# Splitting the last block's V load 3/8 and 5/8 around its K load in a single-core decode attention

## Chip, cores and metric

One core of one Trainium2 chip runs the whole kernel. The metric is the device time of one execution in microseconds (us), as the median of several runs; lower is better. Three runs of the kernel before gave 1286.35, 1285.47 and 1285.8 us, so the median is 1285.8 us.

## What is computed

One token (a row x of 448 numbers) attends to a cache of 65,536 keys. There are 16 query heads and 8 key/value heads of width 256, so each K/V head serves two query heads. A small gated side branch (a layer norm, a gelu and one reduction) is mixed in at the end. Cut to what matters, the reference is:

```python
q = (x @ wq).reshape(B, Sq, 16, 256).transpose(0, 2, 1, 3)
k = jnp.repeat(k_cache, 2, axis=1)            # k_cache: (1, 8, 65536, 256) bf16
v = jnp.repeat(v_cache, 2, axis=1)            # v_cache: the same shape
scores = jnp.einsum("bhqd,bhkd->bhqk", q, k) * (256 ** -0.5)
p = softmax(scores, axis=-1)
o = jnp.einsum("bhqk,bhkd->bhqd", p, v)
a = o.transpose(0, 2, 1, 3).reshape(1, 1, 4096) @ wo
g = sigmoid((x * gate_w).sum(-1, keepdims=True))
return g * a + (1 - g) * b                    # b: the side branch, (1, 1, 448)
```

Almost all bytes are K and V: 8 heads x 65,536 keys x 256 numbers x 2 bytes = 268 MB each.

## The kernel before

**Blocks.** The keys are cut into 32 blocks of 16,384 (four per head), numbered n = 0 to 31 in one loop (line 495); `L` is 31, the last. In a block, each of the 128 partitions holds 128 successive keys ("rows" below, index j). K comes in two halves of 64 rows, 4 MiB each, into two tiles `kn0` and `kn1` (`load_k`, line 106). V comes into one tile `vt` of 128 rows, 8 MiB (`load_v`, line 113). Neither is double-buffered: a tile is loaded again when its last reader is done. All these loads are issued by the SyncE queue (SP) in an order written out by hand.

**Scores of a block** (`score_block`, line 352). A block is 32 groups, t = 0 to 31. A group (`transposes`, line 325) is four TensorE transposes of 128x128 fp32 words (each word is a pair of bf16 numbers) from a K tile into one PSUM bank, and one VectorE copy of that bank to `kT` (line 334). Groups 0 to 15 read `kn0`, groups 16 to 31 read `kn1`. After every fourth group, two batches of four score matmuls (line 343) follow, two and three groups late. `hooks` is a table from t to a function that is called after group t: this is how other work is put among the transposes.

**Softmax** (line 380) is a chain of short steps between VectorE, TensorE and ScalarE. It ends in `p_sb` and its transpose `pT`. There are two `pT` tiles, so block n - 1's may still be read while block n is scored.

**Products with V.** A quarter of a block's products (`pv(n, ip)`, line 366; ip = 0 to 3) is 16 matmuls. Quarter ip reads rows 32 ip to 32 ip + 31 of `vt`. `accumulate` (line 416) then folds the result into `acc` on VectorE.

**Order for ordinary blocks.** Scores of n; issue V of n and both K halves of n + 1; softmax of n; products of n.

**Order around the end.** This is what the change touches. It runs over the last but one block (30) and the last (31):

- After the scores of block 30, SP issues: the first half of V of block 30 (rows 0 to 63), K of block 31 into `kn0` and `kn1`, then the second half of V of block 30 (rows 64 to 127) (lines 511 to 514). Then comes the softmax of block 30, with no products behind it.
- The scores of block 31 carry hooks (line 501): after group 4 a small VectorE step (`result_base`), after group 8 quarter 0 of block 30's products, after group 14 quarter 1.
- V of block 31 is loaded into the K tiles in six pieces of 64, 32, 16, 8, 4 and 4 rows, each as soon as the transposes that read those rows are done (`load_v_last`, line 121).
- After the softmax of block 31 come four small matmuls (line 527), then quarters 2 and 3 of block 30's products (lines 531 and 532), one small matmul (line 533) and `accumulate`.
- Block 31's own products run the other way round (line 552): V is the stationary operand, in 256 short matmuls over the rows j in order. After row 63 the accumulated result `acc` is added by eight fp32 matmuls (`collect`, lines 437 and 559). Then the result is scaled, projected (line 565), copied (line 571) and written out (line 572).

TensorE's instructions run in program order (`seq` writes that order down), and so do SP's issues. The two lines of the order that matter most here:

```python
            score_block(n, {4: result_base, 8: lambda: pv(L - 1, 0), 14: lambda: pv(L - 1, 1)})
...
            load_v(n, 0, KP)
            load_k(L, 0)
            load_k(L, 1)
            load_v(n, KP, VP)
```

Of the kernel before, what the change touches and what calls it, by code (L numbers as in the profile page):

```python
# [20 lines left out]
VP = BLK // 128  # L21
KP = VP // 2
NJ = 16
NI = VP // NJ
# [4 lines left out]
def kernel(  # L29
# [28 lines left out]
    def seq(ins):  # L58
        e = ins.ins.engine
        if e in last:  # L60
            tc.add_manual_dep(
                ins.ins,
                last[e],
                mybir.DependencyInfo(
                    mybir.DependencyClass.NoSync, mybir.DependencyReason.DATA
                ),
                reason="program order",
            )
        last[e] = ins.ins.name
        return ins  # L70
# [31 lines left out]
    def rows(cache, n):  # L102
        g, b = divmod(n, NB)
        return cache[0, g, b * BLK:(b + 1) * BLK, :].rearrange("(p j) d -> p j d", j=VP)

    def load_k(n, h, pieces=((0, KP),)):
        for j0, j1 in pieces:
            seq(nc.sync.dma_start(
                out=k_tiles[h][:, j0:j1, :],
                in_=rows(A_k_cache, n)[:, h * KP + j0:h * KP + j1, :],  # L110
            ))

    def load_v(n, j0=0, j1=VP):
        seq(nc.sync.dma_start(out=vt[:, j0:j1, :], in_=rows(A_v_cache, n)[:, j0:j1, :]))

    def pairs(ap):
        return ap.rearrange("p (i j) d -> p i j d", i=2)
# [3 lines left out]
    def load_v_last(n):  # L121
        for j0, j1 in LAST:
            seq(nc.sync.dma_start(
                out=k_tiles[j0 // KP][:, j0 % KP:(j1 - 1) % KP + 1, :],
                in_=rows(A_v_cache, n)[:, j0:j1, :],
            ))
# [198 lines left out]
    def transposes(i, quarter):  # L325
        tp = tps[state["t"] % 4]
        state["t"] += 1
        for jj in range(4):
            seq(nc.tensor.transpose(  # L329
                tp[:, jj * 128:(jj + 1) * 128],  # L330
                k_tiles[i // 4][:, i % 4 * NJ + quarter * 4 + jj, :].bitcast(FP32),
                ident_f[:, :],
            ))
        seq(nc.vector.tensor_copy(  # L334
            out=kT_tiles[i % 2][:, quarter * 4:(quarter + 1) * 4, :, :].rearrange(
                "p j n c -> p (j n c)"
            ),
            in_=tp[:, :].bitcast(BF16),
        ))

    def scores(g, i, c):
        for a in range(4):
            seq(nc.tensor.matmul(  # L343
                sc_ps[32 * a:32 * (a + 1), :],
                lhsT=qpad[:, c, g, i, :],
                rhs=kT_tiles[i % 2][:, :, 32 * a:32 * (a + 1), c],
                start=(i == 0 and c == 0),
                stop=(i == NI - 1 and c == 1),
                tile_position=(0, 32 * a),
            ))  # L350

    def score_block(n, hooks={}):
        due = []
        for t, (i, quarter) in enumerate((i, q) for i in range(NI) for q in range(4)):
            transposes(i, quarter)
            if due and due[0][0] <= t:
                scores(n // NB, *due.pop(0)[1])
            if quarter == 3:
                due.append((t + 2, (i, 0)))
                due.append((t + 3, (i, 1)))  # L360
            if t in hooks:
                hooks[t]()
        while due:
            scores(n // NB, *due.pop(0)[1])

    def pv(n, ip):
        pT = pT_tiles[n % 2]
        for jj in range(NJ):
            grp = jj % 4
            seq(nc.tensor.matmul(  # L370
                pv_ps[32 * grp:32 * grp + 2 * REP, :, :],
                lhsT=pT[:, 32 * jj + 2 * REP * ip:32 * jj + 2 * REP * (ip + 1)],
                rhs=pairs(vt[:, 32 * ip:32 * (ip + 1), :])[:, :, jj, :],
                start=(ip == 0 and jj < 4),
                stop=(ip == NI // 2 - 1 and jj >= NJ - 4),
                tile_position=(0, 32 * grp),
            ))


    def softmax(n):  # L380
        b = n % NB
        nb, nb_old = nb_tiles[n % 2], nb_tiles[(n + 1) % 2]
        al, pT = al_tiles[n % 2], pT_tiles[n % 2]
        seq(nc.vector.tensor_reduce(out=rmax[:], in_=sc_ps[:, :], op=ALU.max, axis=AXIS.X))  # L384
        seq(nc.tensor.transpose(sm_ps[0:1, 0:128], rmax[:, 0:1], ident_f[:, :]))  # L385
        seq(nc.vector.tensor_reduce(  # L386
            out=(mrun if b == 0 else mnew)[:],
            in_=sm_ps[0:1, 0:128].rearrange("o (a i r) -> o r a i", a=4, r=REP)[:, :, :, 0:NI],
            op=ALU.max, axis=AXIS.XY,
        ))  # L390
        if b > 0:
            seq(nc.vector.tensor_tensor(out=mrun[:], in0=mrun[:], in1=mnew[:], op=ALU.max))  # L392
        seq(nc.tensor.matmul(  # L393
            sm_ps[:, 128:128 + REP], lhsT=ones_f[0:1, :], rhs=mrun[0:1, :], start=True, stop=True
        ))
        seq(nc.vector.tensor_tensor_reduce(  # L396
            out=junk[:], in0=sm_ps[:, 128:128 + REP], in1=nval[:], scale=1.0, scalar=0.0,
            op0=ALU.mult, op1=ALU.add, accum_out=nb[:, 0:1],
        ))
        seq(nc.scalar.activation(  # L400
            out=p_sb[:, :], in_=sc_ps[:, :], func=ACT.Exp, scale=scale,
            bias=nb[:, 0:1], accum_out=den[:, 0:1],
        ))
        if b > 0:
            seq(nc.scalar.activation(
                out=al[:], in_=nb_old[:], func=ACT.Exp, scale=-1.0, bias=nb[:, 0:1]
            ))
        seq(nc.vector.transpose(out=pT[:, :], in_=p_sb[:, :]))  # L408
        if b > 0:
            seq(nc.vector.scalar_tensor_tensor(  # L410
                out=lsum[:], in0=lsum[:], scalar=al[:, 0:1], in1=den[:], op0=ALU.mult, op1=ALU.add
            ))
        else:
            seq(nc.vector.tensor_copy(out=lsum[:], in_=den[:]))
# [52 lines left out]
    L = NBLK - 1  # L467

    def products(n):
        for ip in range(NI // 2):  # L470
            pv(n, ip)
        accumulate(n)
# [22 lines left out]
    for n in range(NBLK):  # L495
        if n == 0:
            score_block(n, {8: gate_sum, 20: mixer_tail})
        elif n < L:
            score_block(n, {5: gate_column, 16: last_wo} if n == 1 else {})
        else:  # L500
            score_block(n, {4: result_base, 8: lambda: pv(L - 1, 0), 14: lambda: pv(L - 1, 1)})
        if n < L - 1:
            load_v(n)
            load_k(n + 1, 0)
            load_k(n + 1, 1)
            if n == 0:
                seq(nc.sync.dma_start(
                    out=wo_sb[:], in_=A_wo.rearrange("(h p c) n -> p h c n", p=128, c=2)
                ))
        elif n == L - 1:  # L510
            load_v(n, 0, KP)
            load_k(L, 0)
            load_k(L, 1)
            load_v(n, KP, VP)
        else:
            load_v_last(L)
        softmax(n)
        if n == L:
            seq(nc.vector.tensor_scalar(
                out=esc[:], in0=fst[:], scalar1=al_tiles[L % 2][:, 0:1], scalar2=None, op0=ALU.mult  # L520
            ))
            seq(nc.vector.tensor_scalar(
                out=lsv[:], in0=val[:], scalar1=lsum[:, 0:1], scalar2=None, op0=ALU.mult
            ))
            f_ps = tps[0][:, 0:NCOL]
            for k in range(NCOL):
                seq(nc.tensor.matmul(  # L527
                    f_ps[:, k:k + 1], lhsT=base[0:1, k, :],
                    rhs=ones_f[0:1, 0:1], start=(k == 0), stop=False, skip_group_check=True,
                ))  # L530
            pv(n - 1, 2)
            pv(n - 1, 3)
            seq(nc.tensor.matmul(
                hd_ps[:, 456:456 + REP], lhsT=ones_f[:, :], rhs=lsv[:, :], start=True, stop=True
            ))
            accumulate(n - 1)
            seq(nc.vector.reciprocal(out=rdv[:], in_=hd_ps[:, 456:456 + REP]))
            seq(nc.vector.tensor_scalar(
                out=rdv[:], in0=rdv[:], scalar1=gcol[:, 0:1], scalar2=None, op0=ALU.mult
            ))  # L540
        if n < L - 1:
            if n % NB == NB - 1:
                denominators()
            products(n)
            if n % NB == NB - 1:
                head_end(n // NB)
# [56 lines left out]
```

## Time and profile before

| what | value |
|---|---|
| median of three runs | 1285.8 us (1285.47 to 1286.35) |
| the profiled execution's own time | 1285.52 us |
| its span in the profile | 1283.7 us |
| mean granted TensorE clock | 0.862 |
| TensorE matmul busy | 975.9 us, 76% |
| VectorE busy | 756.1 us, 59% |
| read from HBM | 544.22 MB, 424 GB/s over the span |
| DMA busy, slices 1 to 39 of 40 | 90% or more each |

The profiled execution lies 0.28 us under the median of the three runs, and 1.8 us of it lie outside the span. The granted clock is the share of full speed at which TensorE was let run; in this trace it is either 1 or 0.5 at any moment. "Landing" is the moment when the last of a load's sixteen completions was recorded. A line such as `kn<-in_A_k_cache_dram` names a load by its destination tile and its source. Lines with L329 are transposes, L343 score matmuls, L370 products of block 30 and earlier, L552 the products of block 31.

### The profile page before, as it was taken

What the parts mean: (1) busy time and instruction counts of PE and PEld (TensorE: products, weight loads), DVE (VectorE), ACT (ScalarE), POOL (GpSimd) and SP (SyncE); (2) the same over time, 40 slices, a digit from 0 to 9 for tenths busy, and PEclk for the clock granted to TensorE, in tenths of its full rate; (3) what the DMA queues carried; (4) which work ended last, traced back from release to release, by engine and by line L of the source; (5) the groups of instructions that cost most, each with busy time, mean ns of one, the idle gap of its engine ahead of it and who ended that gap; (6) DMA issues with size and microseconds to landing.
All of it is one profiled execution on the core that took longest, in us unless ns stands there. A gap on an engine that the chain in (4) does not pass through costs nothing.

```text
span 1283.7 us, 20141 instructions
## 1 busy us (share of the span) xinstructions
PE 975.9 (76%) x8761; PEld 639.8 (50%) x8761; DVE 756.1 (59%) x1360; ACT 44.9 (3%) x111; POOL 6.3 (0%) x9
## 2 busy tenths in 40 slices
PE   5767777787768888777877788877788767878677
PEld 4444444554445554445554455644455444455455
DVE  6565555665556655556654566645576555676563
ACT  4000000000000000000000000000000000000000
POOL 1000000000000000000000000000000000000000
PEclk9888888988888887888887888878889888898887
DMA  9999999999999999999999999999999999999996
GB/s 409 422 430 428 440 419 433 432 435 434 440 418 435 438 434 430 431 427 434 437 436 438 421 430 434 437 432 431 434 427 436 437 437 423 427 420 438 398 403 255
DMA packets 17838, 545.51 MB, mean 425 GB/s; under 512 B 2260, under 2 KB 4310, under 8 KB 4822
## 3 DMA queue, kind: packets, MB, share of 16 engines
q1 hardware_dynamic: 17312, 544.22, 98.6%
q8 instruction: 68, 1.11, 0.3%
q14 instruction: 20, 0.16, 0.0%
q10 hardware_dynamic: 438, 0.01, 0.0%
HBM read 544.22 MB, written 0.00 MB: 424 GB/s over the span
## 4 chain that ended last, share of the span: by engine, by line
DMA 68%; PE 30%; DVE 2%; issue 0%; DVEq 0%
DMA kn<-in_A_k_cache_dram 67%; PE tps L329 23%; PE sc_ps L343 5%; DVE kT L334 1%; PE pv_ps L370 0%; PE hd_ps L552 0%; PE sm_ps L552 0%; DMA xr<-in_A_x_dram 0%; PE tps L527 0%; PE hd_ps L440 0%; PE sm_ps L440 0%; DVE acc L418 0%; DVE rmax L384 0%; DVE z L278 0%; PE tps L565 0%
## 5 line engine op out<-in xcount | busy, mean ns | idle before, releaser
L334 DVE COPY kT<-tps 128x1024 bf16<-128x1024 bf16 x1024 | 647.1, 685 | 184.2 <-PE tps L329 183.2
L329 PE MATMUL tps<-ident_f,kn 128*128 128x128 f32 x4096 | 603.6, 296 | 108.4 <-DMA kn<-in_A_k_cache_dram 108.4
L329 PEld LDWEIGHTS tps<-ident_f,kn 128*128 128x128 f32 x4096 | 486.8, 151 | 228.8 <-DMA kn<-in_A_k_cache_dram 122.0
L370 PE MATMUL pv_ps<-vt,pT 128*4 128x512 bf16 x1984 | 172.9, 524 | 94.6 <-DMA vt<-in_A_v_cache_dram 90.8
L343 PE MATMUL sc_ps<-kT,qpad 128*32 128x512 bf16 x2048 | 201.0, 393 | 28.2 <-DVE kT L334 28.1
L370 PEld LDWEIGHTS <-pT 128*4 128x4 bf16 x1984 | 58.3, 108 | 195.3 <-issue 132.6
L418 DVE SCALAR_TENSOR_TENSOR acc<-acc,al,pv_ps 128x512 f32<-128x512 f32 x23 | 17.2, 748 | 160.5 <-PE pv_ps L370 160.5
L343 PEld LDWEIGHTS <-qpad 128*32 128x32 bf16 x2048 | 52.9, 93 | 110.8 <-issue 101.7
L400 ACT ACTIVATE p_sb<-sc_ps,nb 128x512 bf16<-128x512 f32 x32 | 22.0, 687 | 1178.4 <-DVE nb L396 1178.4
L423 DVE COPY acc<-pv_ps 128x512 f32<-128x512 f32 x8 | 5.5, 692 | 58.6 <-PE pv_ps L370 58.6
L408 DVE STREAM_TRANSPOSE pT<-p_sb 128x512 bf16<-128x512 bf16 x32 | 22.8, 712 | 28.9 <-ACT p_sb L400 28.9
L384 DVE TENSOR_REDUCE rmax<-sc_ps 128x1 f32<-128x512 f32 x32 | 22.1, 691 | 23.2 <-PE sc_ps L343 23.2
L385 PE MATMUL sm_ps<-ident_f,rmax 128*1 128x128 f32 x32 | 8.8, 276 | 25.4 <-DVE rmax L384 25.4
L393 PE MATMUL sm_ps<-mrun,ones_f 1*128 1x2 f32 x64 | 14.1, 288 | 14.2 <-DVE mrun L392 11.7
L385 PEld LDWEIGHTS sm_ps<-ident_f,rmax 128*1 128x1 f32 x32 | 2.5, 79 | 41.5 <-DVE rmax L384 41.5
L393 PEld LDWEIGHTS sm_ps<-mrun,ones_f 1*128 1x128 f32 x64 | 11.4, 221 | 20.4 <-DVE mrun L392 16.5
L396 DVE CUSTOM_DVE_ANT_0 junk<-sm_ps,nval 128x2 f32<-128x2 f32 x32 | 5.1, 159 | 17.1 <-PE sm_ps L393 17.1
L426 PE MATMUL hd_ps<-lsum,same 128*128 128x1 f32 x14 | 4.1, 362 | 13.9 <-DVE lsum L410 13.9
L426 PEld LDWEIGHTS hd_ps<-lsum,same 128*128 128x128 f32 x14 | 3.5, 311 | 14.5 <-DVE lsum L410 14.5
L386 DVE TENSOR_REDUCE mnew<-sm_ps 1x2 f32<-1x64 f32 x24 | 5.1, 213 | 8.9 <-PE sm_ps L385 8.9
L440 PE MATMUL hd_ps<-esc,acc 128*128 128x2 f32 x32 | 5.4, 274 | 6.0 <-DVE acc L418 6.0
L440 PEld LDWEIGHTS hd_ps<-esc,acc 128*128 128x128 f32 x32 | 4.8, 211 | 9.6 <-DVE acc L418 9.6
(99 smaller groups left out, 138.0 us busy)
## 6 DMA issues: line engine op xcount, KB each, us to landing
kn<-in_A_k_cache_dram SPq DMA_DIRECT2D x63, 4096.0 KB, 26.8
vt<-in_A_v_cache_dram SPq DMA_DIRECT2D x2, 4096.0 KB, 27.4
kn<-in_A_k_cache_dram SPq DMA_DIRECT2D x2, 2048.0 KB, 11.7
kn<-in_A_v_cache_dram SPq DMA_DIRECT2D x1, 4096.0 KB, 14.2
wo_sb<-in_A_wo_dram SPq DMA_DIRECT2D x1, 3584.0 KB
vt<-in_A_wq_dram SPq DMA_DIRECT2D x1, 3072.0 KB, 10.4
kn<-in_A_v_cache_dram SPq DMA_DIRECT2D x1, 2048.0 KB, 13.6
kn<-in_A_v_cache_dram SPq DMA_DIRECT2D x1, 1024.0 KB, 13.4
```

The source lines that it names most:

```text
L329: seq(nc.tensor.transpose(tp[:, jj * 128:(jj + 1) * 128], k_tiles[i // 4][:, i % 4 * NJ + quarter * 4 + jj, :].bitcast(FP32), ident_f[:, :],))
L334: seq(nc.vector.tensor_copy(out=kT_tiles[i % 2][:, quarter * 4:(quarter + 1) * 4, :, :].rearrange("p j n c -> p (j n c)"), in_=tp[:, :].bi ...
L343: seq(nc.tensor.matmul(sc_ps[32 * a:32 * (a + 1), :], lhsT=qpad[:, c, g, i, :], rhs=kT_tiles[i % 2][:, :, 32 * a:32 * (a + 1), c], start=( ...
L370: seq(nc.tensor.matmul(pv_ps[32 * grp:32 * grp + 2 * REP, :, :], lhsT=pT[:, 32 * jj + 2 * REP * ip:32 * jj + 2 * REP * (ip + 1)], rhs=pair ...
L384: seq(nc.vector.tensor_reduce(out=rmax[:], in_=sc_ps[:, :], op=ALU.max, axis=AXIS.X))
L385: seq(nc.tensor.transpose(sm_ps[0:1, 0:128], rmax[:, 0:1], ident_f[:, :]))
L393: seq(nc.tensor.matmul(sm_ps[:, 128:128 + REP], lhsT=ones_f[0:1, :], rhs=mrun[0:1, :], start=True, stop=True))
L400: seq(nc.scalar.activation(out=p_sb[:, :], in_=sc_ps[:, :], func=ACT.Exp, scale=scale, bias=nb[:, 0:1], accum_out=den[:, 0:1],))
L408: seq(nc.vector.transpose(out=pT[:, :], in_=p_sb[:, :]))
L418: seq(nc.vector.scalar_tensor_tensor(out=acc[:], in0=acc[:], scalar=al_tiles[n % 2][:, 0:1], in1=pv_ps[:, :, :], op0=ALU.mult, op1=ALU.add,))
L426: seq(nc.tensor.matmul(hd_ps[:, 460:461], lhsT=same[:].rearrange("p a r -> p (a r)"), rhs=lsum[:, 0:1], start=True, stop=True,))
L440: seq(nc.tensor.matmul(o_ps[c], lhsT=acc[:, e, :].rearrange("p (d c) -> p c d", c=2)[:, c, :], rhs=weights[:, e, :], start=(start and e == ...
```

## The change

The first piece of block 30's V load takes 48 rows (3/8 of 128) instead of 64, the second takes 80 rows instead of 64. Quarter 1 of block 30's products reads rows 32 to 63, so it needs both pieces; it is no longer called after group 14 and runs after the softmax of block 31 instead, ahead of quarters 2 and 3. Nothing is computed differently, and no instruction is added or removed: on TensorE, 16 weight loads and 16 matmuls stand later in the order; on SP, two loads have other sizes; the orders of the other engines are the same.

```diff
@@ -498,7 +498,7 @@
         else:
-            score_block(n, {4: result_base, 8: lambda: pv(L - 1, 0), 14: lambda: pv(L - 1, 1)})
+            score_block(n, {4: result_base, 8: lambda: pv(L - 1, 0)})
         if n < L - 1:
             load_v(n)
             load_k(n + 1, 0)
@@ -508,10 +508,10 @@
         elif n == L - 1:
-            load_v(n, 0, KP)
+            load_v(n, 0, 48)
             load_k(L, 0)
             load_k(L, 1)
-            load_v(n, KP, VP)
+            load_v(n, 48, VP)
         else:
             load_v_last(L)
         softmax(n)
@@ -528,8 +528,8 @@
-            pv(n - 1, 2)
-            pv(n - 1, 3)
+            for ip in range(1, NI // 2):
+                pv(n - 1, ip)
             seq(nc.tensor.matmul(
                 hd_ps[:, 456:456 + REP], lhsT=ones_f[:, :], rhs=lsv[:, :], start=True, stop=True
             ))
```

## Prediction

> **What bounds the kernel now.** I read the page's chain first, then the same chain in order of time over the last 80 us, then SP's issues with their times to landing, then the clock in stretches of 2 us, then the timeline of the tail.
>
> The page's shares of the chain say that the transfers bound the kernel:
>
> ```profile
> DMA 68%; PE 30%; DVE 2%; issue 0%; DVEq 0%
> ```
>
> In order of time (start, duration, what), the end of the chain is another matter:
>
> ```profile
> 1215.87 19.33 DMA kn<-in_A_k_cache_dram
> 1235.25 5.38 PE tps L329 x24
> ...
> 1243.06 0.97 PE pv_ps L370 x16
> ...
> 1248.57 0.86 PE pv_ps L370 x16
> ...
> 1265.26 3.35 PE pv_ps L370 x32
> ```
>
> The last DMA in the chain is block 31's first K half, landing at 1215.87 + 19.33 = 1235.20. From there to the end every step is TensorE or what it waits for, so whatever brings that landing forward, or shortens TensorE's work behind it, moves the end. The next view is the tail's timeline (start, duration, engine, line):
>
> ```profile
> 1269.51 0.16 PE L552 MATMUL hd_ps<-pT,kn 128*128 128x2 bf16 x1 [0.63 <-DVE rdv L537]
> ...
> 1272.78 0.99 PE L440 MATMUL hd_ps<-esc,acc 128*128 128x2 f32 x4
> ...
> 1274.28 3.68 PEld L552 LDWEIGHTS <-kn 128*128 128x128 bf16 x128
> ```
>
> Block 31's products start at 1269.51, pause for `collect`, and end at 1274.28 + 3.68 = 1277.96; 5.8 us of scaling, projection and output follow. How far this can move forward is set by the last V pieces. The queue's own timeline gives the issues:
>
> ```profile
> 1215.87 11.16 SPq L108 DMA_DIRECT2D kn<-in_A_k_cache_dram  x2
> 1227.08 0.43 SPq L114 DMA_DIRECT2D vt<-in_A_v_cache_dram  x1
> 1250.05 11.33 SPq L123 DMA_DIRECT2D kn<-in_A_v_cache_dram  x6
> ```
>
> The second and the third of them again, with bytes and time to landing:
>
> ```profile
> vt<-in_A_v_cache_dram SPq DMA_DIRECT2D x1, 4096.0 KB, 27.4
> kn<-in_A_v_cache_dram SPq DMA_DIRECT2D x1, 4096.0 KB, 14.2
> ```
>
> V's second half, issued at 1227.08, lands at 1254.5; block 31's first V piece, issued at 1250.05, at 1264.2; the last piece (issued at 1260.9, 13.4 us to landing on the page) at 1274.3. Last the clock (third column from the right):
>
> ```profile
> 1229.00:1231.00 2.00, 0.51 (x3) 0.29 (x2) 0.53 (x4) 0.70 (x3) 0.00 (x0) 0.92 0.99 381
> 1239.00:1241.00 2.00, 2.00 (x12) 1.33 (x10) 1.84 (x3) 0.00 (x0) 0.00 (x0) 0.52 1.18 508
> 1263.00:1265.00 2.00, 1.43 (x11) 1.24 (x11) 0.56 (x5) 0.48 (x1) 0.00 (x0) 0.96 0.94 401
> 1267.00:1269.00 2.00, 1.88 (x22) 0.59 (x11) 0.37 (x1) 0.00 (x0) 0.00 (x0) 0.69 0.99 416
> 1271.00:1273.00 2.00, 2.00 (x76) 2.00 (x73) 0.00 (x0) 0.00 (x0) 0.00 (x0) 0.66 0.36 134
> ```
>
> As the clock is 1 or 0.5, a mean of 0.92 over 2 us is a step 1.68 us in. So it drops at 1230.68, rises at 1240.92, drops at 1264.84, rises at 1268.24 and drops at 1271.64. The gaps (10.24, 23.92, 3.40, 3.40) are all whole multiples of 3.41: the clock is decided on a grid. TensorE slows after a mostly idle stretch of the grid and recovers after a busy one: idle from 1230.0 to 1235.25, busy from then, full speed only at 1240.92.
>
> **The change, term by term** (against the profiled execution, span 1283.7, own time 1285.52, 0.28 under the median of the runs).
>
> *1. K lands earlier.* 1 MiB of V moves from ahead of K to behind it. From 1235.20 to 1264.2, 12 MiB land (second K half, V's second half, block 31's first V piece): 29.0 / 12 = 2.42 us per MiB. From block 30's first K half (1177.45 + 27.79 = 1205.24) to 1235.20 it is 29.96 / 12 = 2.50. I take **-2.42** (bounds -2.5 and, if the landing is not set by the queue, 0). The queue does set it: the issue at 1215.87 is 19.33 us ahead of landing, the transfer itself takes 9.7, so the issue could slip 9.6 before it mattered, and an opening of 2.42 is inside that. The trace's records of the load's sixteen completions show why the issue time does not matter although the bandwidth dips near 1215: seven engines finish at 1227.4 to 1227.9, eight at 1232.2 to 1233.1, one at 1235.20, and only the last, which never runs dry (its completions follow each other every 9.66 to 10.6 us per 4 MiB), makes the landing.
>
> *2. Quarter 1 leaves the transposes.* On the chain 16 matmuls take **-0.86** (L370 x16 at 1248.57); the other such row, 0.97, is the other bound. Nothing else fills the gap: the twelve transposes on either side follow at their usual pace.
>
> *3. Quarter 1 joins the tail.* 32 matmuls take 3.35 there, at half clock, so 16 cost +1.68 if they run so too, and +0.86 at full clock. On the grid of this trace they run at full clock: everything ahead is earlier by terms 1, 2 and 4, so the products start at 1265.26 - 3.7 = 1261.6 instead of 1265.26. The grid's marks before 1264.84 are 1261.42 and 1258.0; the softmax now idles the stretch 1258.0 to 1261.42, so the clock drops at 1261.42 and rises at 1264.84 after a busy stretch. In the 3.2 us until then 31 matmuls run (3.35 / 32 = 0.105 each); the other 17 take 0.054 each, 0.9. They end at 1265.75; before, the 32 ended at 1268.6. I take **+0.8** on this grid, +1.68 as the other bound.
>
> *4. Clock at the head of block 31.* Before, 5.67 us were slow (1235.25 to 1240.92). Now the transposes start at 1232.83 and the stretch 1234.10 to 1237.51 is the first fully busy one: 4.68 slow. The six groups ahead of the first scores take 5.3 us slow (1235.25 to 1240.55), and 3.23 at full clock in block 30 (1205.29 to 1208.52), so a slow us costs 0.39: **-0.4**. On another grid it is anything from -0.9 to +0.5.
>
> *5. The rest.* Block 31's products start 0.94 after the last of block 30's (1268.57 to 1269.51), unchanged. That puts them at 1266.7. First half 3.25, `collect` 0.9 to 1.72 by the clock, second half 3.3 to 3.48: the end would be 1274.1 to 1275.2. V's later piece (1254.5, unchanged, as the bytes ahead of its end are the same) is long there when quarter 1, which now needs it, runs at 1261.6; were it later, the whole tail would stand behind that wait on TensorE, but the cover is 7 us. But the last V piece lands at 1274.3 as before: its engine works on without a gap from V's second piece (1254.5) to the last one, so an earlier issue brings nothing. Its last 4 rows need 8 matmuls of 0.026: the end cannot come before 1274.5, a gain of 3.4.
>
> The edits to SP's order cost nothing: same number of issues, same waits, 0.33 to 0.43 us each beside running transfers. Group 16 needs `kn1` at about 1246.4; it lands 9.66 after `kn0`, at 1242.4, 4 us of cover.
>
> Sum on this grid: -2.42 - 0.86 + 0.8 - 0.4 = -2.9 at the start of the products, and up to -3.4 at the end if `collect` is at full clock. On the worst grid: -2.42 - 0.86 + 1.68 + 0.5 = -1.1. The runs do not share one grid as far as I can tell, so I shade the value for this grid: **2.8 us**, from the median 1285.8: **1283.0**.
>
> [...]
>
> **Rivals.**
>
> *A: the tail stays slow.* Quarter 1 runs at half clock and `collect` too. For: the 32 products of before did, all but the last. Against: 48 slow products would last 5.0 us, longer than a grid stretch. Gain 2.42 + 0.86 - 1.68 = 1.6, with term 4 between 1.1 and 2.5: **1283.3 to 1284.7**, middle 1284.2.
>
> *B: K does not land earlier.* The change then only moves 16 matmuls: between -0.86 + 0.86 and -0.86 + 1.68, **1285.8 to 1286.6**. For: the bandwidth dips at the issue (262 GB/s at 1213 to 1217), so some engines wait for it. Against: the one that lands last does not.
>
> *C: the other side: the 40 KB rows of the second V piece move badly.* The trace has loads of 8 MiB, 4 MiB and 2 MiB (rows of 64, 32 and 16 KB) but none of 5 MiB. If the 5 MiB took longer than 12.1 us, everything behind it in the queue, all six last pieces, slips by as much. The first 3.4 us of a slip fall into the end's slack; from then on each costs one. Slower by over 0.2% (2.57 us) needs 6 us, a rate a third lower: **1289**. For: nothing measured. Against: 4 MiB pieces keep 2.42 us per MiB, and the 2 MiB piece too (issue to landing puts it 4.85 behind its forerunner).
>
> **How the numbers follow.** Forecast 0.60 (gain 2.2 to 3.4, 1282.4 to 1283.6), A beyond that 0.25, B 0.08, C 0.07. About 0.2% is what a measurement of this kernel can tell from no change, here 2.57 us. That cuts the forecast: I give 0.55 of its 0.60 to more than 2.57, since on this grid the sum is -2.9 to -3.4. Within 0.2%: 0.05 + 0.25 + 0.08 = 0.38; slower: 0.07. The range runs from 1282.2 (the largest gain, 3.4, and 0.2 for the scatter of the runs) to 1285.0 (the worst grid's 1.1 less 0.3 of scatter).
>
> **What would show it.** Term 1: block 31's first transposes 2.4 us earlier, after a shorter DMA in the chain. Term 2: one row L370 x16 among them. Term 3: an L370 row x48 behind softmax, 4.1 us long if right, 5.0 under A. Term 5: a wait for a DMA in the second half of L552, and last landings where they were. It is wrong if K's landing stays, or if the second V piece lands later than it did.

## The result, and the profile after

The changed kernel takes 1283.82 us (median of 22 runs, 1282.54 to 1284.38), the kernel before 1285.95 (22 runs, 1284.99 to 1286.46). The ratio is 0.9983, with a 95% interval from 0.9976 to 0.9990. So the change makes it faster by about 2.1 us, or 0.17%: clear of zero, but inside the 0.2% that the prediction took as "no change". The profiled execution took 1284.01 us, its span is 1282.2.

The page's chain by engine has hardly moved (`DMA 67%; PE 30%`). What the change did shows in the chain in order of time of the changed kernel (start, duration, what):

```profile
1217.84 14.40 DMA kn<-in_A_k_cache_dram
1232.28 5.38 PE tps L329 x24
...
1240.06 0.96 PE pv_ps L370 x16
...
1261.20 4.41 PE pv_ps L370 x48
...
1272.64 0.87 issue
...
```

Block 31's first K half now lands at 1217.84 + 14.40 = 1232.24, 2.96 earlier, although its load is issued 1.97 later. One row of 16 products is left among the transposes, and 48 stand behind softmax. One line is new: 0.87 us of "issue", time in which TensorE waited for nothing that the profile shows. The tail's weight loads show the place (start, duration, engine, line; in brackets the idle time before):

```profile
1266.51 3.33 PEld L552 LDWEIGHTS <-kn 128*128 128x128 bf16 x127 [0.69 <-issue]
...
1271.28 1.28 PEld L552 LDWEIGHTS <-kn 128*128 128x128 bf16 x38
1273.51 2.48 PEld L552 LDWEIGHTS <-kn 128*128 128x128 bf16 x90 [0.95 <-issue]
```

The second half of block 31's products, 128 matmuls in one piece before, stops after 38 of them for 0.95 us. Matmul 38 works on row 64 + 19 = 83, in the middle of the V piece of rows 64 to 95, which had landed at 1269.62. So it is no wait for V.

SP's queue after, with the landing of the two pieces that changed places in size (last column: us from issue to landing):

```profile
1217.84 11.16 SPq L108 DMA_DIRECT2D kn<-in_A_k_cache_dram  x2
1229.05 0.43 SPq L114 DMA_DIRECT2D vt<-in_A_v_cache_dram  x1
1246.18 11.15 SPq L123 DMA_DIRECT2D kn<-in_A_v_cache_dram  x6
```

```profile
vt<-in_A_v_cache_dram SPq DMA_DIRECT2D x1, 5120.0 KB, 25.7
kn<-in_A_v_cache_dram SPq DMA_DIRECT2D x1, 4096.0 KB, 18.6
```

V's second piece lands at 1254.8 and the first piece of block 31's V at 1264.8. Before it was 1254.5 and 1264.2. Block 31's V is issued 3.9 earlier and lands no earlier; the last piece lands at 1274.49 (1274.31 before).

The clock in the changed profile (third column from the right), read as in the prediction, steps at 1237.87, 1261.76 and 1268.59; between the last two it rises at 1265.18 (the row from 1265 to 1267 has a mean of 0.96):

```profile
1237.00:1239.00 2.00, 2.00 (x17) 0.94 (x15) 2.00 (x3) 0.00 (x0) 0.00 (x0) 0.78 1.10 475
1261.00:1263.00 2.00, 2.00 (x26) 0.85 (x29) 1.08 (x4) 0.56 (x3) 0.00 (x0) 0.69 0.78 336
1267.00:1269.00 2.00, 2.00 (x85) 2.00 (x83) 0.00 (x0) 0.00 (x0) 0.00 (x0) 0.90 0.97 412
```

The spacing is 3.41 or a multiple of it again, but the marks lie 0.35 later on the time axis than in the profile before: the grid isn't tied to the start of the span.

Put side by side, from one profile to the other, the sum is:

| stretch | before | after | difference |
|---|---|---|---|
| first transposes of block 31 begin | 1235.25 | 1232.28 | -2.97 |
| transposes of block 31, with what is among them | 25.60 | 24.69 | -0.91 |
| softmax, until the first product behind it | 4.34 | 4.16 | -0.18 |
| products behind softmax (32, 48) | 3.38 | 4.45 | +1.07 |
| until block 31's products | 0.94 | 0.93 | -0.01 |
| their first half and `collect` | 4.98 | 4.98 | 0 |
| their second half | 3.55 | 4.58 | +1.03 |
| end of the products | 1278.04 | 1276.07 | -1.97 |

The span is only 1.5 shorter, as the last transfer, the output, took 4.19 us to land instead of 3.74. The change doesn't touch it.

### The profile page after: what moved, and what is told of

Same layout as the page of the kernel before. It is cut to its first block, busy times and chain, and to the rows that moved or that the text cites. A ratio compares the mean times of both kernels' runs of the same rounds, so it can differ in the third digit from the quotient of the medians.

```text
span 1282.2 us, 20141 instructions
## 1 busy us (share of the span) xinstructions
PE 977.5 (76%) x8761; PEld 638.9 (50%) x8761; DVE 755.8 (59%) x1360; ACT 44.9 (4%) x111; POOL 6.4 (0%) x9
## 3 DMA queue, kind: packets, MB, share of 16 engines
q8 instruction: 68, 1.11, 0.3%
## 4 chain that ended last, share of the span: by engine, by line
DMA 67%; PE 30%; DVE 2%; issue 0%; DVEq 0%
DMA kn<-in_A_k_cache_dram 67%; PE tps L329 23%; PE sc_ps L343 5%; DVE kT L334 2%; PE pv_ps L370 0%; PE hd_ps L552 0%; PE sm_ps L552 0%; DMA xr<-in_A_x_dram 0%; PE tps L527 0%; PE hd_ps L440 0%; PE sm_ps L440 0%; DVE acc L418 0%; DVE rmax L384 0%; DVE z L278 0%; PE tps L565 0%
## 5 line engine op out<-in xcount | busy, mean ns | idle before, releaser
L370 PE MATMUL pv_ps<-vt,pT 128*4 128x512 bf16 x1984 | 176.5, 533 | 97.9 <-DMA vt<-in_A_v_cache_dram 92.2
```

Source lines behind the costliest of these rows:

```text
L370: seq(nc.tensor.matmul(pv_ps[32 * grp:32 * grp + 2 * REP, :, :], lhsT=pT[:, 32 * jj + 2 * REP * ip:32 * jj + 2 * REP * (ip + 1)], rhs=pair ...
```

## The experiments

The theory after the result: K's earlier landing is the gain; moving the quarter costs about what it saves; and the rest is lost in the tail, to the clock, to TensorE's own instructions and, below these, to the last V landing. TensorE's instructions are loaded too. The page's part on queues lists 68 packets of 16 KB in queue 8 (`q8 instruction: 68, 1.11, 0.3%`), and the trace has 17,522 TensorE instructions (8,761 weight loads and as many matmuls): one packet for every 258. I estimate 256 from that (64 bytes each, 16,384 / 256); e3 and e4 below show the count. By the packet records, in the changed kernel such a load begins at 1271.11, and TensorE goes on at 1273.51. In the kernel before it begins at 1271.31, and TensorE gets to the same matmul only at 1275.50.

### e1: the quarter is moved, the V load stays in halves

```diff
-            load_v(n, 0, 48)
+            load_v(n, 0, KP)
...
-            load_v(n, 48, VP)
+            load_v(n, KP, VP)
```

> The kernel before, with quarter 1 behind softmax but the V load still in halves. Theory (the gain is K's earlier landing; moving the quarter itself costs): K lands at 1235.2 as before, the transposes end 0.86 earlier, the tail grows by 0.86 to 1.68, so 0 to 0.8 us slower than before (1285.95 to 1286.8, ratio 1.0000 to 1.0006). Rival (taking products out of the transposes is what gains): about 1.5 to 2 us faster, as the full change is.

Measured: 1285.43 us (11 runs), ratio 0.9997, interval 0.9988 to 1.0006. From the chain of e1 (its first row is the landing of K, unchanged):

```profile
1218.11 17.09 DMA kn<-in_A_k_cache_dram
...
1235.25 4.29 PE tps L329 x24
...
1241.81 0.96 PE pv_ps L370 x16
...
1263.61 5.25 PE pv_ps L370 x48
```

K lands at 1235.20 as before. Moving the quarter alone is worth nothing that can be measured. The rival, by which it is the gain, had 1.5 to 2 us; the interval ends at 1.54 us faster, so only the lowest edge of that is left. The theory's own range, 1285.95 to 1286.8, was missed too, by 0.5 us on the fast side. The row of 48 is 5.25 us long here and 4.41 in the changed kernel: the same 48 products, at half clock throughout in the one, at full clock for the first 0.6 and the last 0.4 us in the other. In this profile the clock was on the other hand up earlier at the head (1238.27): the first 24 transposes took 4.29 us, not 5.38.

### e2: the quarter is late among the transposes

```diff
-            score_block(n, {4: result_base, 8: lambda: pv(L - 1, 0)})
+            score_block(n, {4: result_base, 8: lambda: pv(L - 1, 0), 30: lambda: pv(L - 1, 1)})
...
-            for ip in range(1, NI // 2):
-                pv(n - 1, ip)
+            pv(n - 1, 2)
+            pv(n - 1, 3)
```

> The changed kernel, with quarter 1 after group 30 of block 31 (at about 1255.5, when V's second piece has landed at 1254.8) instead of behind softmax. Block 31's products then start 0.2 to 0.8 us earlier, at 1265.7 to 1266.3, as 16 matmuls cost 0.86 there and 1.06 or more in the tail. Theory (the end waits for TensorE's own next 256 instructions, a 16 KB load that starts only when the last V pieces thin out near 1271.1): the pause in the second half of L552 grows by as much and the time stays within 0.3 us of the changed kernel, 1283.5 to 1284.1. Rival (the end follows TensorE's work, the pause is an accident of the profile): 0.2 to 0.8 us faster, 1283.0 to 1283.6.

Measured: 1283.65 us (11 runs), ratio 0.9984, interval 0.9976 to 0.9993. The time is that of the changed kernel, as the theory had it, but the profile doesn't show the mechanism: on this run's grid the tail was at half clock for 6.8 us, block 31's products began at 1267.09, later than in the changed kernel, and the pause was 0.54, shorter and not longer. For the theory's reason the run is inconclusive, and the rival's 1283.0 to 1283.6 lies inside the interval (1282.7 to 1284.9). Whether the quarter stands ahead of softmax or behind it makes no difference that these runs resolve.

### e3 and e4: tiny matmuls in the prologue move the boundaries of TensorE's instructions

```diff
+    for _ in range(96):
+        seq(nc.tensor.matmul(
+            sm_ps[:, 460:461], lhsT=ones_b[:, :], rhs=ones_b[:, 0:1], start=True, stop=True
+        ))
     seq(nc.vector.tensor_copy(out=xm[:], in_=x_col[:, 0:3]))
```

e4 has 32 instead of 96. They write a column that nothing reads.

> The changed kernel with 96 tiny extra matmuls (96 weight loads, 96 matmuls, 192 TensorE instructions) in the prologue, where TensorE is idle. They move every boundary of 256 instructions back by 192 instructions. Theory (wait for instructions): boundaries in the tail stand at the first matmul of quarter 1 (1261.2), at matmul 78 of L552's first half (1268.5) and at matmul 70 of its second half (1273.4); the first has 7 us for its load, the second 4.9 with the data gone from 1271, so the pause of 0.95 shrinks to 0.2 at most and the time is 0.7 to 1.0 below the changed kernel: 1282.8 to 1283.1, ratio 0.9975 to 0.9978. Rival 1 (the pause is a wait for the last V pieces, which land by 1274.5): pause and time stay, 1283.8. Rival 2 (a step of the clock): the same, 1283.8.

> The same with 32 tiny extra matmuls, 64 instructions. Theory: the boundary moves from matmul 38 of L552's second half to matmul 6 of it, reached at about 1271.6, 4.8 us after the boundary before it at matmul 14 of the first half; the load lags 3 us or more behind a boundary while data flows, so a pause of 0.6 to 1.6 us stands there instead, exactly 32 matmuls earlier, and the time stays within 0.5 us of the changed kernel: 1283.4 to 1284.4. Rivals (last V pieces, clock): a pause stays where it was, near matmul 38.

Measured: e3 1283.56 us (11 runs), ratio 0.9983 (0.9974 to 0.9992); e4 1283.85 us (11 runs), ratio 0.9986 (0.9977 to 0.9995). The tails of e3, then of e4 (four more lines in the source: L552 is L556 here):

```profile
1272.36 2.13 PEld L556 LDWEIGHTS <-kn 128*128 128x128 bf16 x70
1274.73 1.63 PEld L556 LDWEIGHTS <-kn 128*128 128x128 bf16 x58 [0.24 <-issue]
```

```profile
1272.04 0.42 PEld L556 LDWEIGHTS <-kn 128*128 128x128 bf16 x6
1273.41 3.33 PEld L556 LDWEIGHTS <-kn 128*128 128x128 bf16 x122 [0.95 <-issue]
```

The counts decide it: the pause stands after 70 matmuls in e3 and after 6 in e4, where the theory had put it, and after 38 without extra matmuls. That 96 more pairs put it at 38 - 96 + 128 = 70 also shows the period: 128 pairs of weight load and matmul, 256 instructions. (e3's page has 69 of the 16 KB packets, one more than the changed kernel's.) Neither the V pieces nor the clock know of these counts. The pause is TensorE waiting for its next instructions. In all four (changed kernel, e2, e3, e4) it ends 2.2 to 2.4 us after the packet of instructions begins.

The times were a miss for e3. It was to be 0.7 to 1.0 below the changed kernel and is 0.26 below, which the intervals don't separate from zero. In its profile the pause is down to 0.24, but the 48 products took 5.29 us (half clock) instead of 4.45, so in this profile it gave elsewhere what it saved. How much the pause costs in the median is not settled by these runs.

### e5 and e6: products fill softmax's idle time

Block 30's products don't depend on block 31's softmax. e5 puts 24 of the changed kernel's 48 between softmax's TensorE steps; e6 does the same with quarters 2 and 3 of the kernel before. Of e5:

```diff
-    def pv(n, ip):
+    def pv(n, ip, j0=0, j1=NJ):
...
-        for jj in range(NJ):
+        for jj in range(j0, j1):
...
-    def softmax(n):
+    def softmax(n, gaps=(lambda: None, lambda: None)):
...
+        gaps[0]()
         seq(nc.tensor.transpose(sm_ps[0:1, 0:128], rmax[:, 0:1], ident_f[:, :]))
+        gaps[1]()
...
+            softmax(n, (lambda: pv(L - 1, 1), lambda: pv(L - 1, 2, 0, 8)))
...
-            for ip in range(1, NI // 2):
-                pv(n - 1, ip)
+            pv(n - 1, 2, 8, NJ)
+            pv(n - 1, 3)
```

> The changed kernel with the 48 products behind softmax spread: quarter 1 before softmax's first TensorE step, half of quarter 2 before its second, the rest behind it. TensorE then has no idle time of its own in block 31's softmax and its clock stays full. Theory (TensorE's tail is slowed by softmax's idle time, and below that two floors lie: the last V landing, 1274.1 to 1274.7, and the load of TensorE's instructions): block 31's products start near 1263.6 instead of 1266.5; the end stops at the floors, 1274.3 to 1275.9 instead of 1276.1, so 0.2 to 1.8 us below the changed kernel, 1282.0 to 1283.6, and the second half of L552 shows 1 us or more of pauses. Rival (no floor, only TensorE's work counts): 2.9 us below, 1280.9. Rival (the clock plays no part): the same time as the changed kernel or more, 1283.8.

> The kernel before (V in halves, quarters 0 and 1 among the transposes) with quarter 2 before softmax's first TensorE step and half of quarter 3 before its second. Theory: the tail is TensorE's own, at half clock, and nothing lies between it and the end until the floors, 3.4 us away: block 31's products start near 1267.4 instead of 1269.5, and the end comes 1.7 to 3.0 us earlier, 1282.8 to 1284.1, with no earlier K. Rival (K's landing alone sets the end): within 0.4 us of before, 1285.4 to 1286.2.

Measured: e5 1282.89 us (11 runs), ratio 0.9976 (0.9967 to 0.9985); e6 1283.64 us (11 runs), ratio 0.9983 (0.9974 to 0.9992). The clock of e5 in the stretch where it is half in the changed kernel:

```profile
1261.00:1263.00 2.00, 1.76 (x27) 0.73 (x26) 1.61 (x5) 0.39 (x3) 0.00 (x0) 1.00 0.92 393
1263.00:1265.00 2.00, 0.31 (x12) 0.31 (x13) 0.53 (x3) 0.00 (x0) 0.00 (x0) 1.00 1.05 451
```

And e5's weight loads for block 31's products (here L557; the first row is the first half, the others the second):

```profile
1264.69 3.33 PEld L557 LDWEIGHTS <-kn 128*128 128x128 bf16 x128 [2.02 <-DMA kn<-in_A_v_cache_dram]
...
1269.55 1.19 PEld L557 LDWEIGHTS <-kn 128*128 128x128 bf16 x38
1271.06 0.77 PEld L557 LDWEIGHTS <-kn 128*128 128x128 bf16 x26 [0.32 <-issue]
1272.35 0.93 PEld L557 LDWEIGHTS <-kn 128*128 128x128 bf16 x32 [0.51 <-DMA kn<-in_A_v_cache_dram]
1273.60 0.50 PEld L557 LDWEIGHTS <-kn 128*128 128x128 bf16 x16 [0.32 <-DMA kn<-in_A_v_cache_dram]
1274.27 0.29 PEld L557 LDWEIGHTS <-kn 128*128 128x128 bf16 x8 [0.17 <-DMA kn<-in_A_v_cache_dram]
1274.91 0.29 PEld L557 LDWEIGHTS <-kn 128*128 128x128 bf16 x8 [0.35 <-DMA kn<-in_A_v_cache_dram]
```

Block 31's products began at 1264.69, 1.8 earlier than in the changed kernel, and the gain is 0.9 (the intervals of the two overlap). They were to begin near 1263.6. The first row shows why they didn't: TensorE had stood idle for 2.02 us until the first piece of block 31's V landed, at 1264.65. This is a floor that neither the prediction nor the theory had listed. In the changed kernel the piece lands at 1264.76, 1.75 us ahead of its first use, so it hides there; e7 waits 2.11 us for it and e8 1.91. The two floors that had been listed are in the same view: the wait for instructions at matmul 38 (0.32), then four waits for V, each at the first row of a piece (38 + 26 = 64 is row 96, then rows 112, 120 and 124). The last piece landed at 1274.87; TensorE went on at 1274.91 and was done with 8 matmuls. As long as that piece lands there, nothing that TensorE does earlier moves the end.

e6 has no earlier K (its first half lands at 1235.05) and gains 2.2 us all the same, as much as the change. So the kernel before lost about as much to softmax's idle time and the slow clock behind it as to K's landing: from the last transposes to block 31's products it took 8.66 us (1260.85 to 1269.51), and e6 takes 6.30 (1259.92 to 1266.22). Which part of that is hidden work and which is clock, the run doesn't separate. It, too, pauses at matmul 38 (0.60, by "issue").

### e7: one more MiB of V goes behind K

```diff
-            load_v(n, 0, 48)
+            load_v(n, 0, 32)
...
-            load_v(n, 48, VP)
+            load_v(n, 32, VP)
```

> The changed kernel with 32 rows ahead of K and 96 behind, so K's first half lands another 2.4 us earlier (near 1229.8), where TensorE is still in block 30's softmax until 1230; quarters 1 to 3 stay behind softmax. Theory (the gain of an earlier K ends at the floors): block 31's products start 0.5 to 2.4 us earlier, and their pause or their waits for V grow by about as much; 0 to 0.8 us below the changed kernel, 1283.0 to 1283.8. Rival (each MiB behind K is worth 2.4 us of the end less nothing): 2 us or more below, 1281.8 or less.

Measured: 1283.91 us (11 runs), ratio 0.9984 (0.9976 to 0.9993), the time of the changed kernel and 0.1 above the theory's range. K's first half landed at 1230.61. Block 31's products began at 1265.85, only 0.7 earlier than in the changed kernel: the quarters ahead of them were done at 1263.51, but the first piece of block 31's V landed at 1265.80, 1.0 later than there. From e7's second half:

```profile
1272.36 1.70 PEld L552 LDWEIGHTS <-kn 128*128 128x128 bf16 x58 [0.36 <-issue]
1274.47 0.93 PEld L552 LDWEIGHTS <-kn 128*128 128x128 bf16 x24 [0.41 <-DMA kn<-in_A_v_cache_dram]
1275.71 0.29 PEld L552 LDWEIGHTS <-kn 128*128 128x128 bf16 x8 [0.30 <-DMA kn<-in_A_v_cache_dram]
```

The waits for V are there as in e5, and at later times: the last piece landed at 1275.67 (1273.89 to 1274.87 in the others). V's second piece, 6 MiB now, took 15.6 us after K's second half had landed, 2.60 per MiB. So this run shows a small price of the kind that rival C had named, here 1.2 us at the end of the queue. Why this piece is slower per MiB was not tried.

### e8: e5 with the boundaries of e3

This is e5's kernel with e3's 96 matmuls in the prologue.

> e5's kernel with 96 tiny extra matmuls in the prologue, so that the boundaries of 256 TensorE instructions stand at matmul 78 of L552's first half and matmul 70 of its second. Theory: a pause, if there is one, moves to matmul 70 of the second half or 78 of the first, and the end changes by less than 1 us either way against e5, by where the load of those instructions falls among the last V pieces; a wait for V stays at the piece's own first row (matmuls 64, 96, 112, 120 of the second half). Rival (pauses are clock steps or waits for V alone): pauses stay where e5 has them.

Measured: 1282.49 us (9 runs), ratio 0.9975 (0.9966 to 0.9985). Its second half (here L561) has no wait for instructions at all:

```profile
1269.21 1.87 PEld L561 LDWEIGHTS <-kn 128*128 128x128 bf16 x64
1271.71 0.93 PEld L561 LDWEIGHTS <-kn 128*128 128x128 bf16 x32 [0.62 <-DMA kn<-in_A_v_cache_dram]
1272.95 0.51 PEld L561 LDWEIGHTS <-kn 128*128 128x128 bf16 x16 [0.32 <-DMA kn<-in_A_v_cache_dram]
...
1274.26 0.29 PEld L561 LDWEIGHTS <-kn 128*128 128x128 bf16 x8 [0.34 <-DMA kn<-in_A_v_cache_dram]
```

The pause of e5 at matmul 38 is gone, the waits at 64, 96, 112 (0.17) and 120 stay: two kinds of wait, told apart by what moves them. At matmul 70, where the theory had a pause if any, the wait for V at 64 covers it: the packet began at 1269.41, and TensorE got there at 1271.87, 2.46 later. The last piece landed at 1274.22, and the products ended at 1274.64, 0.42 behind it. e8 and e5 are the fastest versions measured, 3.4 and 3.0 us below the kernel before. Between the two the intervals decide nothing.

## Why the prediction was right, and where it was off

The forecast was 2.8 us and the measured gain is 2.1, inside the range and of the forecast sign; 0.38 had been given to "within 0.2%", where it fell, and 0.55 to more. The mechanism of the gain was right: K lands earlier, and e1 shows that without this there is no gain that can be measured. The size was helped by luck. Block 31's products began 3.00 us earlier in the profile, where the sum had -2.9, but the terms missed by -0.54, -0.05, +0.27 and +0.4, and softmax, which was no term, was 0.18 shorter. And 1283.82 lies outside the 1282.4 to 1283.6 that the prediction gave its own mechanism, and inside the 1283.3 to 1284.7 of rival A, which had 0.25. By its terms:

- **1, K lands earlier: right.** -2.42 forecast; -2.96 in the profile. Over the kernels with 48 rows ahead, K's first half landed at 1232.24 to 1233.29, over those with 64 at 1235.05 to 1235.20. Taken by the middle (1232.8 and 1235.1), that is 2.3 for the MiB. Rival B falls; in the changed kernel's records the engine that ends last lands V's first piece 7.26 after K's second half of block 30, and 9.67 before the change.
- **2, the quarter leaves the transposes: right.** -0.86 forecast, -0.91 for the whole stretch.
- **3, the quarter joins the tail: mis-sized.** +0.8 forecast on the old profile's grid; +1.07 in this profile (the row is 4.41, between the 4.1 that was to show and the 5.0 of rival A), and 5.29 for the 48 products in e1 and e3, which is +1.9. Rival A, the slow tail, is thus what some profiles show and others don't.
- **4, the clock at the head: wrong on this grid.** -0.4 forecast, 0 measured: the six groups took 5.38 again. Both terms were worked out on the grid of one profile. Over the ten profiles of this case the marks, counted from the span's start, fall from 0.06 to 3.06 of the 3.41 us. A mean over the grid's places would have been the safer value. By the middle of the prediction's own bounds (+1.24 for term 3, -0.2 for term 4) the sum is -2.2, an estimate.
- **5, the rest: the step that failed.** The end was put at 1274.1 to 1275.2, with no wait but the last V landing below it. The products ended at 1276.07. `collect` ran at half clock (the upper bound), as it does in all ten profiles, and 1.0 us went to a wait for TensorE's instructions, which wasn't among the terms and is on no line of the page before. In the kernel before, the same packet began at 1271.31; if it took the 2.4 us that it took in the changed kernel, it was there 1.8 us ahead of its use at 1275.50, an estimate. "A wait for a DMA in the second half of L552", which was to show, doesn't show in the changed kernel; it does in e5, e7 and e8, 0.04 us behind the landing each time, so the floor was real and lower than the change could reach.

The reading of the clock that terms 3 to 5 rest on, "slows after a mostly idle stretch", is too simple. In the profile before, the clock dropped at 1264.84 after a stretch of the grid in which TensorE was busy 1.92 of 3.41 us, and at 1271.64 after one busy 2.78 of 3.41, most of it with the short matmuls of L552. In the changed kernel it dropped at 1268.59 after a stretch busy 2.79. In e5 it stayed full after stretches busy 2.63 and 2.54. What the clock goes by, these runs don't show.

Rival C didn't happen at 5 MiB: the second piece took 12.1 us after K's second half (1242.67 to 1254.79), 2.42 per MiB. Why the median gained 2.1 and the profile's products 1.97 can be told only in part: the grid differs from run to run, and the pause's share in the median is open.

## What to carry to other kernels

When a chain ends in a tail behind the last load, list every floor under that tail before the gain is counted: the first landing that the tail needs (a wait of 2.02 us in e5) as well as the last, the clock that the tail gets (0.5 from 1264.84 to 1268.24 and from 1271.64 on in the kernel before), and the loads of the engine's own instructions (0.95 us in the changed kernel). Where idle time and independent work lie side by side, put the work into it: in e6 that brought 2.2 us with no earlier K. It hid work, and the clock was full until 1266.40 where before it fell at 1264.84; how much each brought is open. Where the clock's grid lies elsewhere in every profile (here from 0.06 to 3.06 of the 3.41 us), price a term by its mean over the grid and keep the value of the one profile as a bound.

## What the hardware showed that was not expected

TensorE waited for its instructions, 0.95 us of it in the changed kernel. They came in packets of 16 KB over a DMA queue of their own (`q8 instruction: 68` on the page), one for 256 instructions by the shift in e3 (38 - 96 + 128 = 70). In the changed kernel, TensorE passed the boundary before the pause (matmul 46 of the first half) at 1267.66, and the next packet began 3.45 us later, at 1271.11, when the last V pieces were thinning out (379 GB/s from 1269 to 1271, 239 from 1271 to 1273). In the kernel before it passed that boundary at 1270.66 and the packet began 0.64 later. Over the ten profiles this lag was 0.4 to 0.7 where the boundary came at 1270.7 to 1270.9 (before and e1), with the data thinning out (134 GB/s from 1271 to 1273 in the kernel before, after 400), and 2.8 to 3.5 in the other eight, where it came at 1265.8 to 1269.6. That the data holds the packets back is read from these lags; no run tests it alone. While data flowed at full rate (424 GB/s over the span before), the packets of the last ten blocks mostly began 1 to 5 us behind their boundary; nothing waited for them there (the pause is the only idle stretch of TensorE over 0.25 us in the changed profile that no semaphore explains, and the kernel before has none), since 128 pairs of weight load and matmul lasted 12 us or more. In block 31's products they lasted 3.3 (4.8 from boundary to boundary in the kernel before, with `collect` between). There TensorE stood still at a boundary in seven of the ten profiles, for 0.24 to 0.95 us.
